# Weight sums of the first pair's third and fourth unit made one unit at a time, and one norm multiply moved into the second pair

## The chip, the cores and the metric

The kernel runs on one core of a Trainium2 chip, as one launch. The metric is the device time of a launch in microseconds (us), the median of several runs. The engines are called TensorE (PE in the profile: matmuls; PEld is its weight load), VectorE (DVE), ScalarE (ACT), GpSimd (POOL) and SyncE (SP, which here only issues DMAs). Each engine works through its own list of instructions in order; between engines, semaphores hold an instruction until what it reads or overwrites is free.

## The reference

A light convolution over the sequence is followed by a feed-forward block. All is fp32; x is 8 x 4096 x 192, the feed-forward width is 1536.

```python
w = softmax(weight, axis=-1)                       # 8 heads x 7 taps
out[b, s, h, :] = sum_k w[h, k] * x_pad[b, s + k, h, :]   # causal, 24 channels a head
x = out.reshape(32768, 192)
xn = x / sqrt(mean(x * x, axis=-1) + 1e-6) * rms_g
g, val = xn @ w_gate, xn @ w_val                   # 192 -> 1536
y = (g * sigmoid(g) * val) @ w_out                 # 1536 -> 192
```
The four feed-forward arrays arrive as 64-bit floats. The kernel converts them to fp32 itself, out of their 32-bit halves.

## The kernel before, in words

The 32768 tokens are cut into 32 pairs; a pair is two tiles of 512 tokens. The first pair (p = 0) goes a plain way: ordinary products with the gate and value weights in four units of 384 of the 1536 columns (`plain`, line 1118, matmuls on L1139), and then the products with `w_out` (`outer`, L1180). Meanwhile the weights are converted (`convert`: L291 to L331) and linear combinations of them are formed. From the second pair on, a scheme with fewer products is used: 120 products of sums of x with sums of weights in a pair, where the plain way has 144, and then 60 steps for `w_out`. It needs

- sums of the weight slots of each unit: `w_sums(lo, hi)`, 17 sums on POOL (L357) over units lo to hi - 1, in steps of 4, 4, 4, 4 and 1, each ended by a `yield`. Some write new slots (9 to 14), others overwrite slots that the plain products read;
- a sign flip of two slots on ScalarE: `w_signs(lo, hi)` (L367);
- sums of x for each pair: `x_sum` (L712, L719), and two swaps of halves by DMA: `swap` (L701, on SP's queue);
- 17 sums of `w_out`'s slots: `out_sums` (L907, on POOL), each a step of its own.

The first pair's work is ordered by hand. `START` is a string; each letter takes the next step of one stream: `p`, `s`, `v` are a group of six plain products, its SiLU and its multiply; `i` converts a unit's gate and value weights, `o` and `O` convert `w_out`, two steps before and the third with two POOL operations (L322, L323); `c` and `n` are the second pair's convolution and norm; `w` is the next step of `w_sums`. There are 24 `p`, six to a unit. What comes after `START` goes through a queue sorted by a planned place (`put`, `later`, `emit`): the place only decides the order in each engine's list. The places count from `base`, the start of `outer`. The list `LATER` holds the remaining `w` steps, and below it stand the x sums (places 470 to 476), the swaps, the third pair's convolution (`part_tap`, L459 and L467) and norm (`norm(2)`: square, reduce, factor, spread, and `scale`, the multiply on POOL, L537), its stores into a buffer in memory (`place(2)`, L675) and the `out_sums`.

From the second pair on, one list of words, `ORDER`, gives the order of all engines' work in a pair. `p2` means two products (L821; 120 of them in a pair, each of two instructions, and then 60 steps of `w_out` products on L1009). `A`, `V`, `G` and `Q` are ScalarE, VectorE, POOL and a POOL DMA. A word that ends in `-` belongs to the pair before it or prepares the pair after it: `Gmul-` (after product 48) is the next pair's norm multiply and `Dplace-` (after product 68) its stores. In the second pair all such words are passed over, since the first pair did that work in its own way. Nine work tiles (`tile`, `tls`) go round: ScalarE copies a partial sum from PSUM into one (L773), VectorE and ScalarE (SiLU, L867) work on it, and the last multiply, on POOL (L875) or VectorE, gives it free for the next copy. A product that adds to a PSUM bank waits for the copy out of it.

Of the kernel before, what the change touches and what calls it, by code (L numbers as in the profile page):

```python
# [19 lines left out]
def kernel(  # L20
# [333 lines left out]
    def w_sums(lo, hi):  # L354
        t = wf4[:, lo] if hi == lo + 1 else wf4[:, lo:hi]
        for i, (d, op, a, b) in enumerate(WSUM):
            nc.gpsimd.tensor_tensor(  # L357
                out=t[..., d, :], in0=t[..., a, :], in1=t[..., b, :],
                op=ALU.add if op == "add" else ALU.subtract,
            )  # L360
            if i % 4 == 3:
                yield
        yield

    def w_signs(lo, hi):
        t = wf4[:, lo:hi, 6:9:2, :]
        nc.scalar.mul(t, t, -1.0)  # L367
# [182 lines left out]
    def norm(p):  # L550
        for part in (square, reduce, factor, spread, scale):
            part(p)
            yield
# [205 lines left out]
    def put(at, do):  # L759
        heapq.heappush(line, (at, next(tick), do))  # L760
# [500 lines left out]
    def done(it):  # L1261
        for _ in it:
            pass
# [6 lines left out]

    START = (
        "XxxxxxxXdDdDdDddTTTTTTTTaakKkkaaakKkKbkKkbKbbbffpffpfsipsvivpsipisvipsvcpvowsivOcwps"
        "iwpvsicwpsiwvpisvivcpsocvpwispvswcipvwsipsiwOvpsiwvipsvvpsopsvcpsvOnovoOpsonvOpsnoOvnnopso"
    )
    LATER = (
        (30, "s"), (35, "v"), (45, "v"), (47, "O"), (50, "O"), (53, "O"), (60, "t"),
        (463, "w"), (1864, "w"), (1964, "w"), (2064, "w"), (2164, "w"),
    )
    heat(taps[:].rearrange("p h k -> p (h k)"), 1)
    heat(unity, 14)  # L1280
# [14 lines left out]
    for i in range(2, NO):  # L1295
        load_out(i)
    hts = []
    p, sl, v = plain(hts)
# [5 lines left out]
        "O": itertools.chain(*[convert_out(i) for i in range(1, NO, 2)]),  # L1304
        "c": conv(1), "n": norm(1), "t": place(1),
        "p": p, "s": sl, "v": v,
        "w": itertools.chain(*[w_sums(*c) for c in ((0, 1), (1, 2), (2, 4))]),
    }
    for i in START:
        next(pieces[i], None)  # L1310
# [9 lines left out]
    def later(it, *places):  # L1320
        for at in places:
            put(at, functools.partial(next, it, None))
# [17 lines left out]
            at = c + 250 + 100 * k + 50 * j if j < 2 else c + 960 + 80 * k  # L1340
            put(at, functools.partial(part_tap, 2, k, j))
    put(base + 3900, functools.partial(load, 3))
    later(norm(2), c + 1510, c + 1600, c + 1610, base + 2895, base + 2900)
    later(place(2), base + 2905)
    for at, i in zip((470, 471, 472, 474, 475, 476), (0, 3, 2, 1, 4, 22)):
        put(base + at, functools.partial(x_sum, i, "G"))
    put(base + 473, functools.partial(swap, "swA"))
    put(base + 477, functools.partial(swap, "swB"))
    wsum = out_sums()
    later(wsum, *[base + 455 + i for i in range(3)], *[base + 2910 + 10 * i for i in range(14)])  # L1350
    put(base + 470, functools.partial(w_signs, 0, 2))
    put(base + 2660, lambda: nc.scalar.mul(right("p11"), right("p11"), -1.0))
    emit(float("inf"))

# [10 lines left out]
    def last(order, outs):  # L1365

        got, row, n, end = set(), [], 0, []
        todo = [w.split(".")[0] for w in outs]
        late = [w.strip("-") for w in order if w.strip("-")[1:] in NEEDS]

        def settle():
            more = True
            while more:
                more = [w for w in late if got.issuperset(NEEDS[w[1:]].split())]
                for w in more[:1]:
                    late.remove(w)
                    row.append(w)
                    got.add(w[1:])

        def product(k):  # L1380
            row.append("p1")
            todo.remove(k)
            if k not in todo:
                got.add(k)
            settle()

        for w in order:
            if w[-1] == "-":
                row.append(w)
            elif w[0] == "p":  # L1390
                for _ in range(int(w[1:])):
                    n += 1
                    k = outs[n - 121].split(".")[0] if n > 120 else ""
                    if k == "0":
                        end.append(k)
                    elif k:
                        product(k)
                    else:
                        row.append("p1")
            elif w[1:] not in NEEDS:  # L1400
                row.append(w)
                got.add(w[1:])
                settle()
        for k in end:
            product(k)
        assert not late
        return row

    past = None
    for p in range(1, PAIRS):  # L1410
        now, steps = Pair(p), 0
        if p == PAIRS - 1:
            order = last(order, " ".join(OUTS).split())
        for w in order:
            if w[0] == "p":
                for _ in range(int(w[1:])):
                    next(now.line)
                    steps += 1
                    if p == 1 and steps == 40:
                        w_signs(2, 4)  # L1420
                continue
            eng, name = w[0], w[1:]
            of = now
            if name[-1] == "-":
                name, of = name[:-1], past
            if of:
                of.do(eng, name)
        past = now
# [1 line left out]
_INS = ['x', 'weight', 'moe_w_gate', 'moe_w_val', 'moe_w_out', 'moe_rms_g']  # L1430
# [26 lines left out]
```

## Time and profile before

| | us |
|---|---|
| median of 3 runs (lowest, highest) | 2597.13 (2596.12, 2597.48) |
| the profiled execution | 2596.94 |
| its span, first to last instruction | 2595.1 |
| busy: TensorE, VectorE, POOL, ScalarE | 2573.3, 2404.7, 2060.6, 1956.7 |
| first pair: plain products from, `outer` from | 32.4, 94.3 |
| second pair from, third pair from | 125.3, 212.5 |
| a later pair, start to start | 79.0 |

Times in rows are microseconds from the span's start, durations in groups are ns. A row of the order in time reads: start, length, engine, line, operation, output <- inputs, shapes, count, and in brackets how long the engine had been idle and what ended that. A row of waits reads: who <- for whom: us in all, times, longest. A row of one stretch reads: stretch, its length, busy time and instructions of the engine, granted TensorE clock, share of the DMA engines, GB/s. A row of one line's instructions reads: count, shortest/median/longest ns, first to last start.

### The profile page before, as it was taken

The page shows a single profiled execution, that of the slowest core. Times are in us where ns is not written, and L with a number is a line of the kernel's source. Part 1 is how long each engine was busy: PE and PEld are TensorE (multiplying, and loading weights), DVE is VectorE, ACT ScalarE, POOL GpSimd, SP SyncE. Part 2 cuts the span into 40 slices and gives each one's busy share as a digit, 9 for nine tenths or more (in the row PEclk, how much of TensorE's full clock was granted, in tenths as well). Part 3 has the DMA queues.
Part 4 walks back from the last instruction along what each step waited for, and adds up shares of the span by engine and source line. Part 5 has one row for each costly group of instructions (what it writes and reads, how often), then busy time and mean ns, then how long its engine had stood idle before and what let it go on. Part 6 is the DMA issues. An engine that isn't in the chain of part 4 may idle for free.

```text
span 2595.1 us, 61891 instructions
## 1 busy us (share of the span) xinstructions
PE 2573.3 (99%) x23128; PEld 1663.5 (64%) x23128; DVE 2404.7 (93%) x4011; ACT 1956.7 (75%) x3747; POOL 2060.6 (79%) x1564
## 2 busy tenths in 40 slices
PE   8999999999999999999999999999999999999998
PEld 6867666766566666666666676666667666666665
DVE  8879999999999999999999999999999999999976
ACT  6577777887777877778877778777787777787765
POOL 3797778877789777788777797877887777978777
PEclk9999999999999999999999999999999999999999
DMA  6435555545564455555455544555545555544442
GB/s 144 81 73 101 107 100 115 95 90 106 100 115 97 94 103 106 97 115 98 91 102 104 112 103 92 99 108 100 117 93 97 94 109 106 111 91 92 97 96 46
DMA packets 546546, 259.32 MB, mean 100 GB/s; under 512 B 458566, under 2 KB 461126, under 8 KB 546246
## 3 DMA queue, kind: packets, MB, share of 16 engines
q1 hardware_dynamic: 507092, 182.03, 34.5%
q0 software_dynamic: 38192, 73.15, 16.5%
q8 instruction: 182, 2.98, 0.5%
q14 instruction: 118, 0.97, 0.1%
q10 hardware_dynamic: 962, 0.20, 0.0%
HBM read 100.10 MB, written 49.55 MB: 58 GB/s over the span
## 4 chain that ended last, share of the span: by engine, by line
PE 95%; POOL 1%; DVE 1%; DMA 1%; issue 0%; ACT 0%; POOLq 0%; ACTq 0%; SPq 0%; DVEq 0%
PE ps L821 63%; PE ps L1009 29%; PE ps L1139 2%; PE ps L1180 1%; DMA xa<-xd 0%; DVE ps L467 0%; POOL wf L357 0%; POOL x L907 0%; DMA early<-ht 0%; PE ps L406 0%; PE ps L570 0%; DMA xa<-xa 0%; POOL xa L719 0%; DVE ps L1074 0%; POOL yn L537 0%
## 5 line engine op out<-in xcount | busy, mean ns | idle before, releaser
L821 PE MATMUL ps<-xa,wf 64*128 64x512 f32 x7440 | 1648.6, 592 | 6.5 <-ACT tile L773 4.7
L821 PEld LDWEIGHTS ps<-xa,wf 64*128 64x128 f32 x7440 | 1085.3, 187 | 556.3 <-issue 101.6
L773 ACT ACTIVATE tile<-ps 128x512 f32<-128x512 f32 (+1 forms) x770 | 433.3, 570 | 206.4 <-PE ps L1009 108.6
L773 ACT ACTIVATE tls<-ps 128x512 f32<-128x512 f32 (+1 forms) x687 | 386.4, 567 | 168.8 <-PE ps L1009 104.0
L773 ACT ACTIVATE ps<-ps 128x512 f32<-128x512 f32 (+1 forms) x713 | 387.6, 547 | 123.1 <-PE ps L1009 93.2
L875 POOL TENSOR_TENSOR ht<-ht,tile 128x512 f32<-128x512 f32 x305 | 386.6, 1274 | 96.4 <-ACT tile L867 83.7
L1009 PE MATMUL ps<-ht,x 128*32 128x256 f32 x5952 | 390.5, 380 | 2.5 <-DVE o_sb L1022 2.3
L875 POOL TENSOR_TENSOR ht<-ht,tls 128x512 f32<-128x512 f32 x253 | 320.5, 1272 | 64.4 <-ACT tls L867 57.3
L467 DVE SCALAR_TENSOR_TENSOR ps<-xh,tp,ps 128x512 f32<-128x512 f32 x450 | 321.7, 745 | 1.0 <-ACT ps L459 0.9
L1009 PEld LDWEIGHTS ps<-ht,x 128*32 128x32 f32 x5952 | 191.9, 110 | 147.5 <-issue 23.8
L1009 PE MATMUL ps<-early,x 128*32 128x256 f32 x3968 | 254.2, 379 | 0.0
L855 DVE TENSOR_TENSOR tile<-ps,tile 128x512 f32<-128x512 f32 x347 | 236.3, 683 | 16.4 <-ACT tile L773 8.3
L517 POOL TENSOR_TENSOR r<-r,nhalf 128x8 f32<-128x8 f32 x29 | 48.4, 1668 | 241.1 <-ACT r L513 241.1
L855 DVE TENSOR_TENSOR ht<-ps,tile 128x512 f32<-128x512 f32 x325 | 221.1, 683 | 9.9 <-ACT tile L773 6.3
L1030 POOL TENSOR_TENSOR early<-early,ht 128x1024 f32<-128x1024 f32 x93 | 225.4, 2485 | 4.5 <-PE ps L1009 3.4
L867 ACT ACTIVATE tile<-tile 128x512 f32<-128x512 f32 x347 | 215.7, 625 | 2.2 <-DVE tile L855 0.2
L855 DVE TENSOR_TENSOR tls<-ps,tls 128x512 f32<-128x512 f32 x273 | 185.1, 682 | 10.1 <-ACT tls L773 4.2
L1009 PEld LDWEIGHTS ps<-early,x 128*32 128x32 f32 x3968 | 129.1, 110 | 85.2 <-ACT ps L773 5.4
L867 ACT ACTIVATE tls<-tls 128x512 f32<-128x512 f32 x273 | 168.8, 624 | 1.8
L855 DVE TENSOR_TENSOR ht<-ps,tls 128x512 f32<-128x512 f32 x233 | 158.6, 682 | 5.9 <-ACT tls L773 3.5
L1052 POOL TENSOR_TENSOR early<-ht 128x512 f32<-128x512 f32 x124 | 159.6, 1287 | 2.7
L1009 PE MATMUL ps<-early,wo_sb 128*32 128x256 f32 x2232 | 143.8, 379 | 1.0 <-POOL early L1030 0.8
(165 smaller groups left out, 3631.3 us busy)
## 6 DMA issues: line engine op xcount, KB each, us to landing
xa<-xd SPq DMA_DIRECT2D x186, 256.0 KB, 4.2
xa<-xa SPq DMA_DIRECT2D x124, 256.0 KB, 4.2
ht<-ht POOLq DMA_DIRECT2D x31, 1024.0 KB, 8.5
xd<-yn SPq DMA_DIRECT2D x248, 96.0 KB, 2.5
out_dram<-o_sb SPq DMA_DIRECT2D x246, 96.0 KB, 2.0
xh<-in_x_dram SPq DMA_DIRECT2D x192, 105.0 KB, 3.7
xa<-xd SPq DMA_DIRECT2D x124, 128.0 KB, 4.7
more<-ht POOLq DMA_DIRECT2D x62, 256.0 KB, 3.3
```

Of the source, the lines that this page charges most:

```text
L467: nc.vector.scalar_tensor_tensor(out=dst, in0=xk, scalar=w, in1=at, op0=ALU.mult, op1=ALU.add)
L517: nc.gpsimd.tensor_tensor(out=r, in0=r, in1=nhalf[:, 0 : nb * NR], op=ALU.pow)
L773: nc.scalar.activation(out=dst, in_=src, func=AF.Copy, scale=float(s))
L821: nc.tensor.matmul(out=self.new(v, h, True) if first else self.old(v, h), lhsT=wf[self.u][HALF[h], WAT[i], :], rhs=x_op(XOP[i], h), start= ...
L855: nc.vector.tensor_tensor(out=dst, in0=self.old(v, h), in1=t[:], op=plus(s))
L867: nc.scalar.activation(out=t[:], in_=src[:], func=AF.Silu)
L875: engine[eng].tensor_tensor(out=self.hv(v), in0=src, in1=t[:], op=ALU.mult)
L1009: nc.tensor.matmul(out=to[q * Q : (q + 1) * Q, :], lhsT=left[:, u, a], rhs=cols[:, i * HALFT : (i + 1) * HALFT], start=fresh, stop=True, s ...
L1030: nc.gpsimd.tensor_tensor(out=dst, in0=a, in1=b, op=ALU.add)
L1052: engine[eng].tensor_tensor(out=dst, in0=a, in1=b, op=ALU.add)
L1139: nc.tensor.matmul(out=bank(h, bks[h])[:], lhsT=wf[u][HALF[h], AT[h][k] * NF + f, :], rhs=xb[HALF[h], g, k, :], start=(k == 0), stop=(k == ...
L1180: nc.tensor.matmul(out=bank(h, bks[h])[:, w : w + D], lhsT=hts[f // NF][HALF[h], g, f % NF, j * P : (j + 1) * P], rhs=wo_sb[HALF[h], f, :] ...
```

## The change

In `START`, three `w` steps are added after the first group of unit four. The stream `w` now goes unit by unit (0, 1, 2, 3, so 20 steps in place of 15). So 12 of unit three's 17 sums are made during unit four's products, in operations of 128x128 in place of 128x256; its other five and the first eight of unit four's stand between the x sums (places 463, 464, 471, 474), and unit four's other nine at 1864, 1964 and 2064. The x sums and swaps move back by one or two places, with their order kept.

The third pair's multiply is taken out of the queue and made where `Gmul-` stands in the second pair, and its stores where `Dplace-` stands. Ten of the last fourteen `out_sums` stay; four are made in the second pair, after products 36, 40, 44 and 48. The sign flip is made for units one to three early and for unit four after product 40, where it was two and two. `last`, which arranges the last pair, is split into helpers that also take words that `ORDER` does not hold, such as `p1-`: its result is the same.

```diff
@@ -1270,11 +1270,11 @@
 
     START = (
         "XxxxxxxXdDdDdDddTTTTTTTTaakKkkaaakKkKbkKkbKbbbffpffpfsipsvivpsipisvipsvcpvowsivOcwps"
-        "iwpvsicwpsiwvpisvivcpsocvpwispvswcipvwsipsiwOvpsiwvipsvvpsopsvcpsvOnovoOpsonvOpsnoOvnnopso"
+        "iwpvsicwpsiwvpisvivcpsocvpwispvswcipvwsipsiwOvpsiwvipsvvpswwwopsvcpsvOnovoOpsonvOpsnoOvnnopso"
     )
     LATER = (
         (30, "s"), (35, "v"), (45, "v"), (47, "O"), (50, "O"), (53, "O"), (60, "t"),
-        (463, "w"), (1864, "w"), (1964, "w"), (2064, "w"), (2164, "w"),
+        (463, "w"), (464, "w"), (471, "w"), (474, "w"), (1864, "w"), (1964, "w"), (2064, "w"),
     )
     heat(taps[:].rearrange("p h k -> p (h k)"), 1)
     heat(unity, 14)
@@ -1304,7 +1304,7 @@
         "O": itertools.chain(*[convert_out(i) for i in range(1, NO, 2)]),
         "c": conv(1), "n": norm(1), "t": place(1),
         "p": p, "s": sl, "v": v,
-        "w": itertools.chain(*[w_sums(*c) for c in ((0, 1), (1, 2), (2, 4))]),
+        "w": itertools.chain(*[w_sums(*c) for c in ((0, 1), (1, 2), (2, 3), (3, 4))]),
     }
     for i in START:
         next(pieces[i], None)
@@ -1340,15 +1340,15 @@
             at = c + 250 + 100 * k + 50 * j if j < 2 else c + 960 + 80 * k
             put(at, functools.partial(part_tap, 2, k, j))
     put(base + 3900, functools.partial(load, 3))
-    later(norm(2), c + 1510, c + 1600, c + 1610, base + 2895, base + 2900)
-    later(place(2), base + 2905)
-    for at, i in zip((470, 471, 472, 474, 475, 476), (0, 3, 2, 1, 4, 22)):
+    norm2 = norm(2)
+    later(norm2, c + 1510, c + 1600, c + 1610, base + 2895)
+    for at, i in zip((470, 472, 473, 475, 476, 477), (0, 3, 2, 1, 4, 22)):
         put(base + at, functools.partial(x_sum, i, "G"))
-    put(base + 473, functools.partial(swap, "swA"))
-    put(base + 477, functools.partial(swap, "swB"))
+    put(base + 474, functools.partial(swap, "swA"))
+    put(base + 478, functools.partial(swap, "swB"))
     wsum = out_sums()
-    later(wsum, *[base + 455 + i for i in range(3)], *[base + 2910 + 10 * i for i in range(14)])
-    put(base + 470, functools.partial(w_signs, 0, 2))
+    later(wsum, *[base + 455 + i for i in range(3)], *[base + 2910 + 10 * i for i in range(10)])
+    put(base + 470, functools.partial(w_signs, 0, 3))
     put(base + 2660, lambda: nc.scalar.mul(right("p11"), right("p11"), -1.0))
     emit(float("inf"))
 
@@ -1384,23 +1384,36 @@
                 got.add(k)
             settle()
 
+        def products(count):
+            nonlocal n
+            for _ in range(count):
+                n += 1
+                k = outs[n - 121].split(".")[0] if n > 120 else ""
+                if k == "0":
+                    end.append(k)
+                elif k:
+                    product(k)
+                else:
+                    row.append("p1")
+
+        def other(w):
+            if w[1:] not in NEEDS:
+                row.append(w)
+                got.add(w[1:])
+                settle()
+
         for w in order:
             if w[-1] == "-":
                 row.append(w)
             elif w[0] == "p":
-                for _ in range(int(w[1:])):
-                    n += 1
-                    k = outs[n - 121].split(".")[0] if n > 120 else ""
-                    if k == "0":
-                        end.append(k)
-                    elif k:
-                        product(k)
-                    else:
-                        row.append("p1")
-            elif w[1:] not in NEEDS:
-                row.append(w)
-                got.add(w[1:])
-                settle()
+                products(int(w[1:]))
+            else:
+                other(w)
+        for w in order:
+            if w[-1] == "-" and w[0] == "p":
+                products(int(w[1:-1]))
+            elif w[-1] == "-" and "." in w:
+                other(w[:-1])
         for k in end:
             product(k)
         assert not late
@@ -1412,12 +1425,18 @@
         if p == PAIRS - 1:
             order = last(order, " ".join(OUTS).split())
         for w in order:
+            if w[0] == "p" and w[-1] == "-":
+                for _ in range(int(w[1:-1]) if past else 0):
+                    next(past.line)
+                continue
             if w[0] == "p":
                 for _ in range(int(w[1:])):
                     next(now.line)
                     steps += 1
                     if p == 1 and steps == 40:
-                        w_signs(2, 4)
+                        w_signs(3, 4)
+                    if p == 1 and steps in (36, 40, 44, 48):
+                        next(wsum)
                 continue
             eng, name = w[0], w[1:]
             of = now
@@ -1425,6 +1444,10 @@
                 name, of = name[:-1], past
             if of:
                 of.do(eng, name)
+            elif name == "mul":
+                next(norm2)
+            elif name == "place":
+                done(place(2))
         past = now
 # ---- launch: one core; inputs and outputs as the reference has them ----
 _INS = ['x', 'weight', 'moe_w_gate', 'moe_w_val', 'moe_w_out', 'moe_rms_g']
```

## The prediction

> **What bounds the kernel now.** I read the busy table first, then the waits of TensorE, then the chain of waits, then the rows of the stretch that the change touches.
>
> ```profile
> PE 2573.3 (99%) x23128; PEld 1663.5 (64%) x23128; DVE 2404.7 (93%) x4011; ACT 1956.7 (75%) x3747; POOL 2060.6 (79%) x1564
> ```
> ```profile
> PE ps L821 <- ACT tile L773: 4.7, 1, 4.7
> ```
> TensorE is busy 99% of the span, so an edit on another engine pays only where TensorE stands still. Of its waits the longest is one of 4.7 us on a ScalarE copy into a work tile. Next, the products of one pair (line 821, 240 instructions, two to a product): first the second pair, then the fourth, which stands for the undisturbed ones.
>
> ```profile
> L821 PE MATMUL ps<-xa,wf x240: 589/589/1219, 125.3 to 185.9; 64*128 64x512 f32 x120
> ...
> L821 PE MATMUL ps<-xa,wf x240: 589/589/693, 291.7 to 344.2; 64*128 64x512 f32 x120
> ```
> From first to last start the second pair needs 60.6 us, the fourth 52.5. So 8.1 us are lost there, more than the wait of 4.7. The granted clock (the column after TensorE's busy time) accounts for most of the rest:
>
> ```profile
> 143.05:146.47 3.42, 0.56 (x2) 1.00 0.93 167
> 146.47:149.88 3.41, 1.56 (x3) 0.50 1.04 125
> 149.88:153.29 3.41, 3.41 (x10) 0.50 0.42 53
> ```
> After a stretch with 0.56 us of work in 3.42 the clock is 0.50 for 6.8 us. TensorE works in 1.56 + 3.41 = 5.0 of them, at half speed, which is 2.5 us lost: 4.7 + 2.5 = 7.2, and 0.9 is left for the products that settle in around it. Who is late? The chain of waits (start, length, what):
>
> ```profile
> 133.30 2.91 POOL yn L537
> ...
> 146.38 1.27 POOL ht L875
> 147.67 0.61 ACT tile L773
> 148.32 2.07 PE ps L821 x2
> ```
> The second pair's first multiply on POOL (L875) starts at 146.38, behind weight sums, the norm multiply for the third pair (L537) and fourteen output-weight sums that stand ahead of it in POOL's order. The tile that it frees is the one that ScalarE's copy, and then TensorE, stand waiting for.
>
> **The change part by part.** *Ahead of the second pair.* POOL's order before, from the fourth unit of the first pair on:
>
> ```profile
> 69.93 1.53 POOL L322 TENSOR_TENSOR xa<-xa,o_sb 128x384 f32<-128x384 f32 x1
> 81.04 1.00 POOL L323 TENSOR_TENSOR wo_sb<-xa 128x384 f32<-128x384 f32 x1 [9.58 <-DVE xa L316]
> 82.00 2.53 POOL L322 TENSOR_TENSOR xa<-xa,o_sb 128x384 f32<-128x384 f32 x1
> ...
> 88.52 1.02 POOL L322 TENSOR_TENSOR xa<-xa,tls 128x384 f32<-128x384 f32 x1 [2.43 <-ACT tls L314]
> ```
> ```profile
> L357 POOL TENSOR_TENSOR wf<-wf 128x128 f32<-128x128 f32 x34 | 27.3, 816 | 41.1 <-DVE wf L331 35.9 <-PE ps L1139 3.5
> ```
> ```profile
> L357 POOL TENSOR_TENSOR wf<-wf x34: 449/624/1972, 37.5 to 69.1; 128x128 f32<-128x128 f32 x34
> ```
> ```profile
> 32.43 61.89 PE ps L1139 x273
> ```
> ```profile
> L357 POOL TENSOR_TENSOR wf<-wf x4: 728/730/732, 105.7 to 108.0; 128x256 f32<-128x256 f32 x4
> ```
> Twelve of unit three's 17 sums now run ahead of the row at 69.93. The 34 one-unit sums of this phase took 449 to 1972 ns, 816 in the mean, which I take: 12 x 0.82 = 9.8 us. Five write free slots and run at once. The others write slots that unit three's products still read. A group of products takes 61.89 / 24 = 2.6 us; they end at 94.3, the last six are unit four's, so unit three's end at 94.3 - 15.5 = 78.8. POOL waits for its fifth group, read to two thirds at about 75.5, and before the last three sums for 78.8. The last ends at about 81.5. The output-weight conversion behind it (L322, L323, then both again: 1.5 + 1.0 + 2.5 + 1.0 = 6.0) ends at 87.5, before the row at 88.52, for which POOL waited 2.43 us for ScalarE. The 9.58 us of idle time hide the sums: 0 at this price. If that cover is gone, the first norm's multiply, its transfers and the second pair's start all come late (rival three).
>
> VectorE's conversion of unit four's weights may stretch beside a busy POOL; that would delay TensorE before a wait, priced next, that ends at a time of its own. It adds nothing.
>
> *Among the x sums.* Between 105 and 121 POOL did four two-unit sums, then the x sums:
>
> ```profile
> 105.65 3.03 POOL L357 TENSOR_TENSOR wf<-wf 128x256 f32<-128x256 f32 x4
> 109.00 1.27 POOL L719 TENSOR_TENSOR xa<-xa 128x512 f32<-128x512 f32 x1 [0.32 <-DMA xa<-xd]
> 111.57 2.62 POOL L719 TENSOR_TENSOR xa<-xa 128x512 f32<-128x512 f32 x2 [1.30 <-DMA xa<-xd]
> 115.82 2.62 POOL L719 TENSOR_TENSOR xa<-xa 128x512 f32<-128x512 f32 x2 [1.63 <-DMA xa<-xd]
> 118.52 2.35 POOL L712 TENSOR_TENSOR xa<-xa 128x1024 f32<-128x1024 f32 x1
> ...
> 123.27 10.03 POOL L357 TENSOR_TENSOR wf<-wf 128x256 f32<-128x256 f32 x13
> ```
> The two-unit sums ran undisturbed here (728 to 732), so for one unit I take the undisturbed end, 0.45, and 0.04 between two: 0.49. Five of them (2.5) replace the four (3.0) at no cost. Four come behind the first x sum and four behind the third. The fourth x sum then starts at 109.00 + 1.3 + 2.0 + 2.7 + 2.0 = 117.0 less overlaps, say 116.8, where it started at 115.82: of 4.0 us, the idle 1.30 and 1.63 hide 3.0, and 1.0 is left. All behind it is 1.0 late, the second swap among them, for which SP's queue waits. Its DMA and TensorE's rows at the hand-over:
>
> ```profile
> L701 SPq DMA_DIRECT2D xa<-xa x4: 590/616/662, 114.2 to 121.6; - x4
> ...
> DMA to landing us min/median/max: 4.1/4.1/4.1
> ```
> ```profile
> 125.47 0.65 PE L1180 MATMUL ps<-wo_sb,ht 64*128 64x192 f32 x3
> 125.85 17.76 PE L821 MATMUL ps<-xa,wf 64*128 64x512 f32 x79
> ```
> The swap lands at 121.6 + 4.1 = 125.7; the second product reads it and starts when the last L1180 leaves its rows, about 126.0. Landing at 126.7, it holds TensorE by **0.7 us** (bounds: 0, if the sums fit the idle time; 1.5 with 624 ns a sum).
>
> ScalarE's sign flip now covers unit three too and waits for the five sums:
>
> ```profile
> 102.34 0.61 ACT L367 ACTIVATE wf<-wf 128x512 f32<-128x512 f32 x1
> ...
> 107.90 0.48 ACT L1188 COPY o_sb<-ps 128x384 f32<-128x384 f32 x1 [4.37 <-POOL wf L357]
> ```
> It moves to about 107.2, takes 0.9 with half as much again, and behind it wait a tap copy and the evacuation, which goes from 107.9 to about 109; ScalarE was idle 4.37 us there, so 0. The flip at product 40 shrinks.
>
> *The queue ahead of the second pair.* After the last x sum (now 121.9) and the norm's 2.4 us, POOL had 13 two-unit sums (10.0), the multiply (2.9) and 14 output-weight sums of the same 128x256 shape (14 x 0.74 = 10.4). Now it has nine one-unit sums (9 x 0.49 = 4.4) and ten of 0.74 (7.4): 121.9 + 2.4 + 4.4 + 7.4 = 136.1, where it was 146.38. **The 8.1 us go.**
>
> *Inside the second pair.* Four sums (0.74 each, 2.9 together) now stand at products 36, 40, 44 and 48, and the multiply at 48. The fourth pair's rows at that place show POOL's slack:
>
> ```profile
> 307.29 1.26 POOL L875 TENSOR_TENSOR ht<-ht,tls 128x512 f32<-128x512 f32 x1
> 308.86 1.27 POOL L875 TENSOR_TENSOR ht<-ht,tls 128x512 f32<-128x512 f32 x1 [0.30 <-ACT tls L867]
> 310.07 0.91 POOL L1050 DMA_DIRECT2D more<-ht  x1
> 310.99 2.90 POOL L537 TENSOR_TENSOR yn<-y,s 128x1536 f32<-128x1536 f32 x1
> ...
> 315.26 1.27 POOL L875 TENSOR_TENSOR ht<-ht,tls 128x512 f32<-128x512 f32 x1 [0.21 <-DVE ht L855]
> 316.90 1.27 POOL L875 TENSOR_TENSOR ht<-ht,tile 128x512 f32<-128x512 f32 x1 [0.38 <-DVE ht L855]
> ```
> ```profile
> 319.14 0.59 ACT L867 ACTIVATE tile<-ps 128x512 f32<-128x512 f32 x1
> ...
> 320.77 0.59 ACT L773 ACTIVATE ps<-ps 128x512 f32<-128x512 f32 x1
> ```
> Ahead of the multiply POOL has 0.3 us of idle time, so it runs 2.9 - 0.3 = 2.6 us behind an undisturbed pair from there on. Of that, 0.21 and 0.38 of idle time behind it take back 0.6. The multiply at 316.90 ends at 318.17 and frees the tile for ScalarE's SiLU at 319.14, so the tile lay ready for 1.0: the SiLU comes 1.0 late. So does, in ScalarE's order behind it, the copy into a bank for unit three (320.77 to 321.36), which product 70 needs. That product stands at 291.73 + 69 x 0.4375 = 321.92, so the copy had 0.5 us to spare: TensorE waits **0.5 us** (bounds: 0, and 2.6, the whole lag). Other tiles that I walked lie ready for longer.
>
> *SP's queue.*
>
> ```profile
> 136.23 5.24 SPq L675 DMA_DIRECT2D xd<-yn  x8
> ```
> The third pair's eight stores (5.2 us of issue) move into the second pair, behind the multiply, which ends some 3 us later in its pair than elsewhere; the fetches that read them stand near the end of the products, as in all later pairs. The last output store of the first pair and the fourth pair's load, queued behind the stores before, now go ahead of them; nobody waits for either: 0.
>
> **Sum.** The profiled execution took 2596.94 us, 0.2 below the median of the runs. 2596.9 - 8.1 + 0.7 + 0.5 = 2590.0; for a median I say 2590.2.
>
> One rule speaks against the change: the Trainium skill, GPSIMD Engine Reference, Key points, says that POOL shares its SBUF interfaces with VectorE and contends with VectorE operations that have two SBUF inputs. By that rule, the trace agrees: a sum took up to 1972 ns against 449. With every added sum at the slow end the time by the rule would be that of rival three.
>
> **The rivals.**
> 1. *The wait only moves into the second pair.* The 2.6 us of lag reach TensorE whole. By the clock rows, a mostly idle stretch costs half of one or two of 3.41 us more, say 2.5: 2596.9 - 8.1 + 0.7 + 2.6 + 2.5 = 2594.6. For it: tiles are what TensorE waited for. Against: the lag sits between other work, with tiles lying ready.
> 2. *The swap comes late by the full eight sums.* 4.0 us of wait and 2.5 of clock: 2596.9 - 8.1 + 4.0 + 2.5 + 0.5 = 2595.8. Against: the 1.30 and 1.63 of idle time. The Trainium skill, TensorE: Matmul & The Clock Gate, Why this matters for your kernels, puts the limit for idle gaps at some 3 us; this one would exceed it. Rival one's would not, and by that rule it would come to 2592.1.
> 3. *Slower: the twelve sums block the first norm.* At 1.97 each they take 23.6 us, where 88.5 - 69.9 - 6.0 = 12.6 fit beside the conversions. The multiply, its stores, the fetches and the swap come 11 late: 2596.9 - 8.1 + 11 + 2.5 + 0.5 = 2602.8. From 1.5 us a sum on (18 - 12.6 + 2.5 of clock) it eats the whole gain. Against: the mean of 0.82 in the same phase.
> 4. *It does nothing*: the late tile has a second cause. The chain shows POOL without a break, so hardly: 2597.
>
> **How the numbers follow.** The forecast 0.71 (2588.8 to 2593: both waits at their lower ends, or most of their upper), rival one 0.10, two 0.06, three 0.09, four 0.04. 0.2% of 2597 is 5.2 us, about what can be told from no change, so faster begins below 2591.9. Of the forecast's 0.71, 0.04 lie above that. Faster 0.67, same 0.24, slower 0.09. The range 2588.6 to 2595 takes in the forecast and rival one.
>
> **What would show it.** Right: no wait of TensorE on L773 near 143; a clock of 1.00 throughout 143 to 153; POOL's first L875 near 137; a wait of under 1 us on the swap at 126; products of the second pair from first to last start in 53 to 54 us. Wrong: the row of 88.52 and the multiply behind it late on POOL; a clock of 0.50 near 128; a wait on L773 past product 60.

## The result and the profile after

The changed kernel took 2589.63 us, the median of eight runs (2588.97 to 2591.99), and the kernel before 2597.43 beside it (eight runs, 2596.12 to 2598.85). The ratio is 0.9972, with a 95% interval of 0.9961 to 0.9982: faster by 4.7 to 10.1 us. The profiled execution took 2589.41 us with a span of 2587.6, which is 7.5 less than the span before. Seven more runs of it, beside the last experiment, hold one of 12377.34 us, for which no trace shows a cause.

The busy table after, and then the products of the second and of the fourth pair (count, shortest/median/longest ns, first to last start):

```profile
PE 2571.1 (99%) x23128; PEld 1642.3 (63%) x23128; DVE 2405.7 (93%) x4011; ACT 1957.8 (76%) x3747; POOL 2069.4 (80%) x1581
```
```profile
L821 PE MATMUL ps<-xa,wf x240: 589/589/693, 125.8 to 179.3; 64*128 64x512 f32 x120
...
L821 PE MATMUL ps<-xa,wf x240: 589/589/693, 284.8 to 337.3; 64*128 64x512 f32 x120
```
POOL has 17 instructions more and is busy 8.8 us longer. The time is not made there: the second pair's products now take 53.5 us from first to last start where they took 60.6, and 52.5 in an undisturbed pair. Their longest matmul is back at 693 ns from 1219, the mark of half the clock. The same three stretches of TensorE as before, with the granted clock behind the busy time:

```profile
143.05:146.47 3.42, 3.42 (x19) 1.00 0.00 0
146.47:149.88 3.41, 3.41 (x19) 1.00 0.44 77
149.88:153.29 3.41, 3.41 (x18) 1.00 0.23 47
```
TensorE's wait of 4.7 us on L773 is gone from the list of waits, and the two half-speed stretches with it. POOL's order after, from unit four of the first pair to the second pair's first multiply, and the moved multiply itself:

```profile
58.66 16.74 POOL L357 TENSOR_TENSOR wf<-wf 128x128 f32<-128x128 f32 x17 [3.01 <-PE ps L1139]
76.04 4.92 POOL L357 TENSOR_TENSOR wf<-wf 128x128 f32<-128x128 f32 x7 [0.64 <-PE ps L1139]
80.91 1.33 POOL L322 TENSOR_TENSOR xa<-xa,o_sb 128x384 f32<-128x384 f32 x1
...
86.09 1.00 POOL L323 TENSOR_TENSOR wo_sb<-xa 128x384 f32<-128x384 f32 x1
89.04 1.01 POOL L322 TENSOR_TENSOR xa<-xa,tls 128x384 f32<-128x384 f32 x1 [1.95 <-ACT tls L314]
...
109.47 1.27 POOL L719 TENSOR_TENSOR xa<-xa 128x512 f32<-128x512 f32 x1 [0.90 <-DMA xa<-xd]
...
117.09 2.62 POOL L719 TENSOR_TENSOR xa<-xa 128x512 f32<-128x512 f32 x2
...
124.54 4.49 POOL L357 TENSOR_TENSOR wf<-wf 128x128 f32<-128x128 f32 x9
...
136.34 1.28 POOL L875 TENSOR_TENSOR ht<-ht,tile 128x512 f32<-128x512 f32 x1
...
147.84 3.14 POOL L537 TENSOR_TENSOR yn<-y,s 128x1536 f32<-128x1536 f32 x1
```
The weight sums now run through unit four, with one wait of 0.64 for the plain products. The row that stood at 88.52 stands at 89.04 and still waits 1.95 us for ScalarE. The fourth x sum starts at 117.09, and the first L875 at 136.34 in place of 146.38.

The second swap, and behind it on SP's queue the fourth pair's load and the third pair's stores:

```profile
L701 SPq DMA_DIRECT2D xa<-xa x4: 591/618/662, 115.2 to 122.9; - x4
...
DMA to landing us min/median/max: 4.1/4.1/4.1
```
```profile
127.68 7.32 SPq L156 DMA_DIRECT2D xh<-in_x_dram  x8
151.00 5.23 SPq L675 DMA_DIRECT2D xd<-yn  x8
```
The swap's last transfer is issued at 122.9, 1.3 us later than before, and lands at 127.0.

Where did the 7.5 us come from, place by place? The second pair begins 0.5 later (125.3 to 125.8) and ends 6.6 earlier (185.9 to 179.3), so its products give 7.1 and the hand-over takes back 0.5. The remaining 0.9 stands behind the second pair: 0.5 is spread over the pairs up to the last product (2559.2 to 2552.1, so 7.1 by then), 0.2 of it in the third pair (52.7 us of products before, 52.5 after), and 0.4 lies in the end behind it. A run shown below has that end 1.6 us longer than here with the same work in it, because the clock fell there, so this 0.9 is not put down to the change.

### The profile page after: what moved, and what is told of

Same layout as the page of the kernel before. It is cut to its first block, busy times and chain, and to the rows that moved or that the text cites. A ratio compares the mean times of both kernels' runs of the same rounds, so it can differ in the third digit from the quotient of the medians.

```text
span 2587.6 us, 61902 instructions
## 1 busy us (share of the span) xinstructions
PE 2571.1 (99%) x23128; PEld 1642.3 (63%) x23128; DVE 2405.7 (93%) x4011; ACT 1957.8 (76%) x3747; POOL 2069.4 (80%) x1581
## 4 chain that ended last, share of the span: by engine, by line
PE 97%; DVE 2%; issue 0%; DMA 0%; ACT 0%; POOL 0%; POOLq 0%; ACTq 0%; SPq 0%; DVEq 0%
PE ps L821 63%; PE ps L1009 29%; PE ps L1139 2%; PE ps L1180 1%; DVE ps L467 1%; DMA xa<-xd 0%; PE ps L406 0%; PE ps L570 0%; DVE ps L1074 0%; DVE y L467 0%; POOL early L1052 0%; DVE xa L719 0%; DVE o_sb L1022 0%; POOLq L1475 0%; ACT sq L586 0%
## 5 line engine op out<-in xcount | busy, mean ns | idle before, releaser
L821 PEld LDWEIGHTS ps<-xa,wf 64*128 64x128 f32 x7440 | 1067.0, 186 | 567.0 <-issue 115.6
L773 ACT ACTIVATE tile<-ps 128x512 f32<-128x512 f32 (+1 forms) x770 | 433.5, 570 | 198.3 <-PE ps L1009 108.7
L773 ACT ACTIVATE tls<-ps 128x512 f32<-128x512 f32 (+1 forms) x687 | 386.4, 567 | 169.9 <-PE ps L1009 104.0
L773 ACT ACTIVATE ps<-ps 128x512 f32<-128x512 f32 (+1 forms) x713 | 387.7, 547 | 121.4 <-PE ps L1009 92.6
L875 POOL TENSOR_TENSOR ht<-ht,tile 128x512 f32<-128x512 f32 x305 | 387.5, 1279 | 93.8 <-ACT tile L867 81.2
L875 POOL TENSOR_TENSOR ht<-ht,tls 128x512 f32<-128x512 f32 x253 | 321.5, 1277 | 63.3 <-ACT tls L867 55.3
```

Of the source, the lines that this page charges most:

```text
L773: nc.scalar.activation(out=dst, in_=src, func=AF.Copy, scale=float(s))
L821: nc.tensor.matmul(out=self.new(v, h, True) if first else self.old(v, h), lhsT=wf[self.u][HALF[h], WAT[i], :], rhs=x_op(XOP[i], h), start= ...
L875: engine[eng].tensor_tensor(out=self.hv(v), in0=src, in1=t[:], op=ALU.mult)
```

## The experiments

The theory is one of POOL's queue: whatever stands ahead of the second pair's first L875 counts by its length, whichever of the three parts it belongs to (the multiply, unit three's sums, the four output sums), and once the L875 comes early enough nothing more is gained. A first rival is that the transfers do it: the DMA engines were busy to 0.93 and 1.04 in the half-idle stretches before, with the third pair's eight stores among what was moved away. A second rival is that one part alone carries the gain and the others are there for nothing.

All results, with the second pair's products (first start / us from first to last start) and the first L875:

| kernel | median us | ratio to before [95%] | products | L875 | behind the pair's start | us over 52.4 |
|---|---|---|---|---|---|---|
| before | 2597.43 | | 125.3 / 60.6 | 146.4 | 21.1 | 8.2 |
| after | 2589.63 | 0.9972 [0.9961, 0.9982] | 125.8 / 53.5 | 136.3 | 10.6 | 1.1 |
| multiply and stores moved only | 2594.27 | 0.9986 [0.9976, 0.9996] | 125.9 / 57.7 | 144.3 | 18.4 | 5.3 |
| stores moved only | 2597.23 | 1.0000 [0.9991, 1.0009] | 126.1 / 61.1 | 147.2 | 21.1 | 8.7 |
| unit sums only | 2592.98 | 0.9983 [0.9973, 0.9992] | 126.3 / 55.1 | 142.6 | 16.3 | 2.7 |
| output sums moved only | 2595.54 | 0.9992 [0.9983, 1.0002] | 126.2 / 58.4 | 144.3 | 18.1 | 6.0 |
| after, output sums ahead again | 2589.79 | 0.9969 [0.9956, 0.9981] | 125.7 / 53.0 | 139.3 | 13.6 | 0.6 |
| after, multiply ahead again | 2590.42 | 0.9972 [0.9961, 0.9983] | 125.5 / 53.8 | 139.0 | 13.5 | 1.4 |
| after, sums spread otherwise | 2589.87 | 0.9969 [0.9957, 0.9980] | 125.7 / 52.4 | 138.8 | 13.1 | 0 |
| after, nine sums more ahead | 2596.63 (one run) | | 126.7 / 59.1 | 144.4 | 17.7 | 6.7 |
| sums spread, four of them later | 2589.82 | 0.9973 [0.9963, 0.9982] | 125.8 / 52.5 | 139.0 | 13.2 | 0.1 |
| after, once more | 2589.74 | 0.9971 [0.9959, 0.9982] | 125.8 / 53.5 | 136.3 | 10.6 | 1.1 |

Each ratio is to runs of the kernel before on the same chip, whose medians were 2597.21 to 2598.16. Products are differences of starts given to 0.1 us; by unrounded starts the two versions with the sums spread take 52.46, as an undisturbed pair does. The absolute starts also hold how early the first pair got going, which differs by up to 1.6 us from trace to trace (first plain product at 28.5 to 30.1), so the hand-over is taken further down as the time from the last plain product to the second pair.

**Only the multiply and its stores moved** (an edit of the kernel before):

```diff
-    later(norm(2), c + 1510, c + 1600, c + 1610, base + 2895, base + 2900)
-    later(place(2), base + 2905)
+    norm2 = norm(2)
+    later(norm2, c + 1510, c + 1600, c + 1610, base + 2895)
...
+            elif name == "mul":
+                next(norm2)
+            elif name == "place":
+                done(place(2))
```


> The kernel before with one part of the change: the norm multiply and its stores made in the second pair. Theory A (POOL's time ahead of the second pair's first multiply sets the wait): L875 starts 2.8 us earlier, at about 143.6; it was answered by TensorE 1.9 us later, so the wait at product 41 shrinks from 4.7 to about 2, and a second wait of about 2 comes at products 47 and 48, whose tiles POOL frees late; about 2593.5. Theory B (what held the second pair was the eight stores and the load of x that ran beside it): the wait is gone, about 2590.

Its wait of TensorE, and its stretches as above:

```profile
PE ps L821 <- ACT tile L773: 2.1, 1, 2.1
```
```profile
144.21:147.63 3.42, 1.23 (x4) 1.00 0.00 0
147.63:151.04 3.41, 3.41 (x10) 0.50 0.00 0
151.04:154.45 3.41, 3.41 (x18) 1.00 0.44 77
```
The gain is 2.9 us of products. The wait of 4.7 shrinks by 2.6 to 2.1, as the L875 comes 2.7 earlier in its pair (18.4 for 21.1). The second wait that was expected at products 47 and 48 did not come. One stretch of 3.41 us at half the clock is left of two. DMA is idle in both stretches, and yet TensorE stands still and loses its clock: the stall needs no transfer.

**Only the stores moved** (of the kernel before; the multiply stays ahead of the pair):

```diff
-    later(place(2), base + 2905)
...
+            elif name == "place":
+                done(place(2))
```


> The kernel before with the eight stores alone moved into the second pair, the multiply left where it was. Theory A: POOL's order ahead of the pair is the same, so the wait of 4.7 us, the clock of 0.50 and about 2597 stay. Theory B (the stores and the load of x held the pair): most of the gain is here, about 2591.

```profile
PE ps L821 <- ACT tile L773: 4.8, 1, 4.8
```
```profile
134.06 2.94 POOL L537 TENSOR_TENSOR yn<-y,s 128x1536 f32<-128x1536 f32 x1
...
147.18 1.26 POOL L875 TENSOR_TENSOR ht<-ht,tile 128x512 f32<-128x512 f32 x1
```
```profile
144.75:148.16 3.41, 0.00 (x0) 1.00 0.00 0
```
Nothing is gained: the wait is there in full, behind the same POOL work up to 147.18, and in the stretch in which no matmul runs the DMA engines are idle too (0.00). The rival of the transfers falls.

**Only the unit sums** (the changed kernel, with multiply, stores and all fourteen output sums ahead again):

```diff
-    norm2 = norm(2)
-    later(norm2, c + 1510, c + 1600, c + 1610, base + 2895)
+    later(norm(2), c + 1510, c + 1600, c + 1610, base + 2895, base + 2900)
+    later(place(2), base + 2905)
...
-    later(wsum, *[base + 455 + i for i in range(3)], *[base + 2910 + 10 * i for i in range(10)])
+    later(wsum, *[base + 455 + i for i in range(3)], *[base + 2910 + 10 * i for i in range(14)])
...
-                    if p == 1 and steps in (36, 40, 44, 48):
-                        next(wsum)
...
-            elif name == "mul":
-                next(norm2)
-            elif name == "place":
-                done(place(2))
```


> The changed kernel with the multiply, its stores and all fourteen output-weight sums ahead of the second pair again: of the change only the weight sums one unit at a time are left. Theory A: POOL's first L875 starts 5.7 us later than in the changed kernel, at about 142.1, which product 41 just meets (0.2 us of wait) and products 47 and 48 do not (about 2); nothing is left to do for POOL inside the pair, so no wait at product 70. About 2591.2. Rival (each of the three parts is needed, or the old wait with its clock loss comes back): above 2594.

```profile
143.96:147.37 3.41, 3.30 (x14) 1.00 0.99 116
147.37:150.78 3.41, 3.31 (x12) 1.00 0.34 49
```
The largest single part: 5.5 us of the products' 7.1. Of the waits on L773 one of 0.3 us is left, and the clock stays at 1.00, though only 14 and 12 matmuls ran in stretches that hold 18 or 19 elsewhere. DMA was busy to 0.99 in the first of them, as in the stall before. The L875 came 16.3 us behind the pair's start, and the products lose 2.7.

**Only the four output sums moved** (of the kernel before):

```diff
-    later(wsum, *[base + 455 + i for i in range(3)], *[base + 2910 + 10 * i for i in range(14)])
+    later(wsum, *[base + 455 + i for i in range(3)], *[base + 2910 + 10 * i for i in range(10)])
...
+                    if p == 1 and steps in (36, 40, 44, 48):
+                        next(wsum)
```


> The kernel before with one part of the change: four output-weight sums made after products 36, 40, 44 and 48. Theory A: L875 starts 2.9 us earlier, at about 143.4, the wait at product 41 is about 2, but two of the four sums then stand ahead of the multiplies that products 47 and 48 need: about 3 us more there. About 2595. Theory B: no change, 2597.

```profile
144.85:148.27 3.42, 1.87 (x6) 1.00 0.95 120
148.27:151.68 3.41, 3.41 (x9) 0.50 0.97 120
```
A wait of 1.8 us on L773 and one stretch at half the clock; 2.2 us of products gained. By time alone the ratio's interval just takes in 1. The three parts alone gain 2.9, 5.5 and 2.2 in the products, 10.6 together, where all at once gain 7.1: each shortens the same stall, and what is gone can't be taken away twice. So the second rival falls too: each part gains by itself in the products, though the whole time shows the gain clear of 1 only for the first two. The largest leaves 2.7 us, so it isn't enough alone.

**The output sums put back ahead** (of the changed kernel):

```diff
-    later(wsum, *[base + 455 + i for i in range(3)], *[base + 2910 + 10 * i for i in range(10)])
+    later(wsum, *[base + 455 + i for i in range(3)], *[base + 2910 + 10 * i for i in range(14)])
...
-                    if p == 1 and steps in (36, 40, 44, 48):
-                        next(wsum)
```


> The changed kernel with one part undone: all fourteen output-weight sums stand ahead of the second pair again, the multiply stays inside. Theory A (POOL's time; what stands in the pair matters only if POOL was not idle there anyway): the first L875 starts at about 139.3 in place of 136.3, still 2 us before product 41 needs its tile; POOL's 1.5 us of idle time before its second L875 goes, the multiply comes 1.5 us earlier, and the wait at product 70 goes with it. The second pair's products take 53.0 us from first to last start in place of 53.5; about 2589.1. Rival (the four sums had to leave): a wait at product 41 to 48, 54 us or more.

ScalarE's rows past product 60 of the changed kernel, and then of this one:

```profile
153.37 1.08 ACT L773 ACTIVATE tile<-ps 128x512 f32<-128x512 f32 x2 [1.42 <-POOL ht L875]
154.60 0.60 ACT L867 ACTIVATE tile<-ps 128x512 f32<-128x512 f32 x1
...
156.24 0.59 ACT L773 ACTIVATE ps<-ps 128x512 f32<-128x512 f32 x1
```
```profile
152.45 1.28 ACT L773 ACTIVATE tile<-ps 128x512 f32<-128x512 f32 x2 [0.44 <-PE ps L821]
153.62 0.59 ACT L867 ACTIVATE tile<-ps 128x512 f32<-128x512 f32 x1
...
155.26 0.59 ACT L773 ACTIVATE ps<-ps 128x512 f32<-128x512 f32 x1
```
The products take 53.0, as expected, 0.5 less than after. In the changed kernel ScalarE waits 1.42 us for a multiply of POOL, and the copy into the bank goes 1.0 later; here it waits for TensorE alone. So the four sums inside the pair cost those 0.5 us at product 70. In the whole time this does not show (2589.79 against 2589.63): this is the run whose end is long, 37.1 us from the last product's start (2550.9) to the end of the span (2588.0), where the changed kernel has 35.5. Both ends hold the same last wait of TensorE and the same 32 matmuls behind it, here the changed kernel's and then this one's:

```profile
2581.02 1.93 PE L1009 MATMUL ps<-ht,x 128*32 128x256 f32 x32 [2.26 <-DVE o_sb L1022]
```
```profile
2579.83 3.53 PE L1009 MATMUL ps<-ht,x 128*32 128x256 f32 x32 [2.26 <-DVE o_sb L1022]
```
The granted clock was 1.00 over the first 32 and 0.50 from 2580.00 to 2583.42 over the second: 1.6 us for the same work, the whole difference of the ends. The traces with the stores only and with the unit sums only have such a long end too (37.0 and 37.3 us, with a stretch at 0.50 in it).

**The multiply and stores put back ahead** (of the changed kernel; the words for the multiply and the stores go too, as with the unit sums):

```diff
-    later(norm2, c + 1510, c + 1600, c + 1610, base + 2895)
+    later(norm(2), c + 1510, c + 1600, c + 1610, base + 2895, base + 2900)
+    later(place(2), base + 2905)
```


> The changed kernel with one part undone: the multiply and its stores ahead of the second pair again, the four output-weight sums inside. Theory A: the first L875 at about 139.1, in time for product 41; from the place of the multiply on POOL is level with an undisturbed pair, so no wait at product 70. 53.0 us in place of 53.5, about 2589.1. Rival (the multiply had to leave): a wait at product 41 to 48, 54 us or more.

```profile
142.81 0.73 POOL L907 TENSOR_TENSOR x<-wo_sb 128x256 f32<-128x256 f32 x1
143.62 0.73 POOL L907 TENSOR_TENSOR x<-x,wo_sb 128x256 f32<-128x256 f32 x1
144.30 1.27 POOL L875 TENSOR_TENSOR ht<-ht,tls 128x512 f32<-128x512 f32 x1
145.53 1.27 POOL L875 TENSOR_TENSOR ht<-ht,tile 128x512 f32<-128x512 f32 x1
```
53.8 where 53.0 was expected. The expectation left out that with the L875 at 139.0 two output sums still stand ahead of the next multiplies at 144.30 and 145.53, one of which frees the tile that products 46 to 49 need: 0.8 us of delay there. The place of the sums costs as much as their number.

**The sums spread otherwise**: one step of four unit sums out from between the x sums, and the four output sums out of the products (two ahead again, two among the steps for the output).

```diff
-        (463, "w"), (464, "w"), (471, "w"), (474, "w"), (1864, "w"), (1964, "w"), (2064, "w"),
+        (463, "w"), (464, "w"), (471, "w"), (1864, "w"), (1964, "w"), (2064, "w"), (2164, "w"),
...
-    later(wsum, *[base + 455 + i for i in range(3)], *[base + 2910 + 10 * i for i in range(10)])
+    later(wsum, *[base + 455 + i for i in range(3)], *[base + 2910 + 10 * i for i in range(12)])
...
-                    if p == 1 and steps in (36, 40, 44, 48):
+                    if p == 1 and steps in (140, 150):
```


> A version meant to beat both: the changed kernel, but the four sums of unit four that stood behind the third x sum come after all x sums, twelve output-weight sums ahead of the second pair, and the last two after products 140 and 150, far from the multiply. Theory A: no x sum waits behind weight sums for longer than its transfer, so the second swap is on time; the first L875 at about 139.5; no wait at product 70. 52.7 us for the products in place of 53.5, about 2588.8. Rival (some other wait sets the hand-over and product 70): 53.3 or more.

```profile
L821 PE MATMUL ps<-xa,wf x240: 589/589/693, 125.7 to 178.1; 64*128 64x512 f32 x120
```
```profile
L701 SPq DMA_DIRECT2D xa<-xa x4: 590/618/662, 115.4 to 121.8; - x4
```
52.4: the second pair is undisturbed. The swap's last transfer is issued at 121.8, where the run with the output sums ahead has it at 122.9 as the changed kernel does, and takes 53.0. Of what sets these two apart, the swap is what comes late at the pair's start, and the trace with 53.0 has lost its 0.5 us by product 10 and loses nothing behind it, so some 0.5 us are the swap's price. So the multiply in its new place costs nothing by itself, and neither does an L875 that comes 13.1 us behind the start.

**Nine sums more ahead of the pair** (the changed kernel plus nine operations of 0.8 us, start to start; they write into a slot what the next output sum writes there anyway):

```diff
+    for i in range(9):
+        put(base + 3100 + i, lambda: nc.gpsimd.tensor_tensor(
+            out=right("p14"), in0=right("00"), in1=right("02"), op=ALU.add))
```


> The changed kernel with nine more sums on POOL ahead of the second pair, each the same as one that is made later (the result is the same). It asks for a wait between those seen so far: the first L875 at about 143.0, TensorE idle for some 0.9 us at product 41, and about 3 us more lost in small waits up to product 48. The clock: the trace of before and the single parts showed 0.50 after a stretch of 3.41 us that was busy for 0.56, 1.23 and 1.87 us; if half of a stretch decides, the clock stays at 1.00 here, and the products take about 57 us; if any wait of 1 us costs the clock, 58.5.

```profile
PE ps L821 <- ACT tile L773: 0.9, 1, 0.9
```
```profile
144.85:148.26 3.41, 2.37 (x8) 1.00 0.00 0
148.26:151.68 3.42, 3.42 (x11) 0.50 0.00 0
```
Bare time on POOL, with no data that anybody needs and no transfer (DMA share 0.00), brings the loss back: 59.1 us of products, 5.6 more than after, and the half clock. That is the theory of the queue by itself, though the size was not met (57 or 58.5 were expected). The longest wait in one piece was only 0.9 us, and still the clock fell: the products around it were starved as well, with 8 matmuls in the stretch.

**Four of the sums in unit four moved behind the weight conversion** (an edit of the spread version). The hand-over from the first pair to the second had become 0.5 longer in every version with unit three's sums in unit four. The theory was that POOL's conversions of `w_out`, late by those sums, hold it up.

```diff
-        "iwpvsicwpsiwvpisvivcpsocvpwispvswcipvwsipsiwOvpsiwvipsvvpswwwopsvcpsvOnovoOpsonvOpsnoOvnnopso"
+        "iwpvsicwpsiwvpisvivcpsocvpwispvswcipvwsipsiwOvpsiwvipsvvpswwopsvcpsvOwnovoOpsonvOpsnoOvnnopso"
```


> E7 with one step moved: of the twelve sums in unit four, the last four come behind the second output-weight conversion on POOL. Theory (the hand-over to the second pair is 0.5 us late in every kernel with the twelve sums, 96.65 us after the first plain product in place of 96.12, because the conversions on POOL come late and VectorE's short operations wait beside them): POOL's conversions run at their old times, VectorE's two operations on line 291 and 299 too, and the hand-over is at 96.2 to 96.3. Rival (the longer weight conversion of VectorE for unit four is the cause): 96.6 as in E7. The products of the second pair stay at 52.5 in both.

VectorE's conversion of unit four's weights (L331) and the plain products (L1139), which end where the hand-over begins: before, after and in this run, two rows each:

```profile
L331 DVE SCALAR_TENSOR_TENSOR wf<-xa,rg_sb x3: 628/631/631, 77.5 to 78.6; 128x384 f32<-128x384 f32 x3
```
```profile
L1139 PE MATMUL ps<-xa,wf x288: 589/589/693, 29.2 to 94.3; 64*128 64x512 f32 x144
```
```profile
L331 DVE SCALAR_TENSOR_TENSOR wf<-xa,rg_sb x3: 748/806/807, 77.5 to 78.9; 128x384 f32<-128x384 f32 x3
```
```profile
L1139 PE MATMUL ps<-xa,wf x288: 589/589/693, 29.1 to 94.2; 64*128 64x512 f32 x144
```
```profile
L331 DVE SCALAR_TENSOR_TENSOR wf<-xa,rg_sb x3: 746/805/1369, 76.9 to 78.3; 128x384 f32<-128x384 f32 x3
```
```profile
L1139 PE MATMUL ps<-xa,wf x288: 589/589/693, 28.5 to 94.0; 64*128 64x512 f32 x144
```
From the last plain start to the second pair's first it is 31.0 us before, 31.6 after and 31.8 here. Counted from the first plain product (29.2 before; the 32.4 of the first table is where they begin to run without a break), the second pair begins 96.1, 96.7 and 97.3 us later. It should have become shorter. But the edit did not make what the theory asks for: POOL's conversion in the row of 88.52 starts 59.3 us behind the first plain product before, 59.9 in the spread version and 60.4 here. So the theory of POOL's conversions is not tested by this run.

The traces show another wait, which fits the rival of the expectation, VectorE's longer conversion. TensorE's weight load for unit four's products waits for L331; the list of waits from 76 to 97 us, after and in this run:

```profile
PEld ps L1139 <- DVE wf L331: 0.7, 2, 0.4
```
```profile
PEld ps L1139 <- DVE wf L331: 1.3, 2, 0.9
```
All eight traces with unit three's sums in unit four have it, seven with 0.7 us and this one with 1.3, and a hand-over of 31.5 to 31.8. The four without (before, the multiply and stores, the stores, the output sums) have none there, and 31.0. L331 is longer wherever the sums run beside it: 804 to 807 ns at the median against 610 to 631, and one of 1369 here. By the Trainium skill, GPSIMD Engine Reference, Key points, the two engines share their SBUF interfaces, and there is contention with VectorE instructions that have two SBUF inputs, as L331 has; these rows agree. How the wait carries through the products with `w_out` to the second pair is not walked here, and no run keeps the sums and spares L331, so that this wait makes the whole 0.5 us is likely but not shown.

**The changed kernel once more**, beside the last run, as a measure of what can be told apart:

> The changed kernel itself, on the same chip as E9, for the comparison of the two times. Both theories: 7.5 us below the kernel before; E9 about 1.4 us below it.

2589.74 against 2589.82; 1.4 us less were expected of the last run. No version here is faster than the changed kernel by a difference that these runs can tell; those with 0.5 to 1.0 us less in the second pair do not show it in the whole time, where the end alone differs by 1.6 us between traces.

## Why the prediction was right

2590.2 was forecast and 2589.63 measured, faster as forecast. By its steps:

- *The 8.1 us go.* Right, by the mechanism named: L875 at 136.34 (136.1 forecast), no wait, clock at 1.00. The runs with one part each show the stall shrinking in step with the work that leaves POOL's queue, and the nine added sums bring it back.
- *The twelve sums in unit four cost 0.* Half right. POOL's side came out within 0.6 us: sums to 80.96 (81.5), conversion to 87.1 (87.5), the next row still waiting for ScalarE, so rival three falls. But the step said that a slower VectorE "adds nothing", since the swap would be waited for anyway. Mis-sized there: from the last plain product to the second pair it takes 0.5 longer wherever the sums run in unit four, and TensorE's weight load then waits 0.7 us for that conversion of VectorE, which the swap did not cover.
- *The swap costs 0.7.* The fourth x sum started at 117.09 (116.8 forecast) and the swap landed at 127.0 (126.7). It cost about 0.5, by the two runs without output sums among the products, with and without the step at 474 (53.0 and 52.4). The pair itself began 0.5 late, so the landing was covered by that much more; the two together cost 1.0 where 0.7 was forecast.
- *ScalarE's sign flip costs 0.* Right, at its place (forecast 107.2, 0.9 long, and the evacuation near 109):

```profile
107.52 0.84 ACT L367 ACTIVATE wf<-wf 128x768 f32<-128x768 f32 x1 [4.69 <-POOL wf L357]
...
108.88 0.47 ACT L1188 COPY o_sb<-ps 128x384 f32<-128x384 f32 x1
```
- *Product 70 waits 0.5.* Right: 53.5 against 53.0, and the copy that ends the wait goes 1.0 later on ScalarE, of which 0.5 was to spare. The wait stands one instruction earlier than named, at the copy (L773) ahead of the SiLU.
- *SP's queue costs 0.* Right as far as shown: the stores begin at 151.00 and the load at 127.68, and the third pair's products take 52.5 (205.8 to 258.3).
- *The sum.* 2596.9 - 8.1 + 0.5 (hand-over) + 0.5 (swap) + 0.5 (product 70) = 2590.3, where 2590.0 was worked out and 2589.4 profiled. What makes up the difference is the 0.9 behind the second pair that no step holds. The forecast is right by its large term; its small ones were off by 0.5 and less, in directions that partly cancel, so that the total came within 0.6 us is partly luck.
- *Rival one* did not come, and the lower of its two prices was the less likely one. By the Trainium skill, TensorE: Matmul & The Clock Gate, Why this matters for your kernels, it is idle gaps over some 3 us that cost the clock in mid-kernel. In these runs the longest gap was 2.1, 1.8 or 0.9 us where the clock was lost in the second pair, and one of 2.26 at the kernel's end lost it in one run and kept it in another. The measurement decides. Had the lag reached TensorE whole, the dearer figure of 2594.6 would probably have been the nearer of the two; no run tests that.

## What to carry to other kernels

Where two regimes of a kernel meet, look at the helper engine's order just ahead of the meeting: work there that nobody needs soon delays the first instruction of the new regime by its whole length, and it can go earlier into idle time or later into slack. Such gains do not add: single parts were worth 2.9, 5.5 and 2.2 us, all of them 7.1, and beyond a first multiply some 13 us into the pair more bought nothing. Filling one engine's idle time with work is not free for its neighbour: 12 sums that all fit in POOL's idle time still made the hand-over 0.5 us longer.

## What was not expected of the hardware

In the second pair, a stretch of 3.41 us in which TensorE was busy for 0.00, 0.56, 1.23, 1.87 or 2.37 us was followed by one at a clock of 0.50 in every run that had one; stretches with 3.30 us (14 matmuls) and 3.31 us (12) were not. For these products the limit lies between, so a stretch with nearly a third of its time idle is already past it.

That is no limit for other matmuls. In the changed kernel's end two stretches in a row with 1.71 and 1.93 us of shorter matmuls (from 2576.57 and from 2579.98) were both followed by a clock of 1.00. With the output sums ahead, one there with 0.99 us was followed by 0.50. The wait in them is the same, 2.26 us: the edge at 2579.98 cuts it in two in the first kernel, and in the second it lies whole in the stretch that ends at 2580.00. So neither the length of a gap nor the busy time alone decides; where a gap falls among the stretches seems to count, and what exactly is counted stays open.

In the runs with a wait of 2.1, 1.8 or 0.9 us the clock came back after one such stretch. Where the stretch at half the clock was itself not filled (1.56 us busy before, 2.44 with the stores only), it took two. So the loss grows in a step: with unit sums only, an L875 16.3 us behind the pair's start costs 2.7 us, and with nine sums more ahead one at 17.7 costs 6.7.
